# Packed attention and two feed-forwards on one core: a table moved, latents loaded once, and three pieces of work put in another order

## The chip, the core and the metric

One core of one Trainium2 chip runs the whole program. The metric is device time in microseconds (us) of one execution; 0.2% of it (3.5 us) is about what a measurement of this kernel can tell from no change. The engines are TensorE (PE; weight loads are listed apart as PEld), VectorE (DVE), ScalarE (ACT), GpSimd (POOL) and SyncE (SP), which here only issues DMAs, in the order in which the program writes them.

## The reference

```python
# q, k, v: (8, 8, 576, 64); p: (8, 8, 32, 64); all float32
p_packed = sm_attn(p, k, v)                 # 32 latents per head read 576 keys
out = sm_attn(q, p_packed, p_packed)        # 576 queries read the 32 latents
x = out.transpose(0, 2, 1, 3).reshape(4608, 512)
xn = x / sqrt(mean(x * x) + 1e-6) * rms_g   # first feed-forward, d_ff 1536
g = xn @ w_gate
x1 = (g * sigmoid(g) * (xn @ w_val)) @ w_out
h = x1 @ w_in                               # second feed-forward, d_ff 2048
return (h * cos(h)) @ w2_out
```

The weights arrive as 64-bit floats. The kernel narrows them itself: it loads each value as two 32-bit halves and puts a 32-bit float together from them (one ACT operation, then four DVE operations, or one of POOL and three of DVE).

## The kernel before

Every large product is made of three matmuls (helper `mm3`, L150 to L153): both operands are split into a rounded high part and the rest (`hilo`, L100 to L102: the high part on ACT, the rest on DVE), and high times high, high times low and low times high are added up in PSUM.

**Latent stage** (loop at L573, 18 steps `i`, two per batch and two to drain). Step i loads what later steps need (`load_k`: the latents p and the keys; `load_v`), transposes p and k on PE (`u_prep`, `u_kt`), makes scores, exponentials and the packed latents (`u_s1`, `u_e`, `u_et`, `u_pp`), and `u_fin` multiplies them by rms_g into `ppT` (L444). `u_prep` transposes a tile `pn` that holds p twice side by side; `load_k` fills both halves with a DMA each (L332, L333). Beside this each step loads weights (`w_load`, with `B0_L` for some more), narrows those loaded a step before (`w_prep`: part 0 is the ACT operation, part 1 the DVE ones), runs up to three steps of batch 0's attention (`bg0_step`, 34 of them, `attend(0)`), and at three steps builds a merged weight (`unit`). The last two narrowings, of weight pieces 14 and 15, stand at step 16, and the last `u_fin` at step 17. When the loop ends, its PSUM pools are handed over: the attention's transposes that follow (tile `atp`, L263) write banks that wait for the last reader of the old tiles.

**First feed-forward** (loop at L775). Per batch 24 steps `i`: `gv_block` (12 matmuls of 288 columns for gate and value, tiles `gv`), sigmoid on ACT, two products on DVE (`silu`, L675, L676), the split into `shl`, and two steps later `acc_block` (12 matmuls, tiles `acc`). Four PSUM tiles `mm` are shared by gate and value, the attention and the merged weights. Between these, `att_step` runs the next batch's attention in 41 small steps spread over the 48 half steps of a batch (for batch 0 from `ATT_FROM0` on), `U_AT` says after which step which merged weight `(batch, unit)` of batches 0 and 1 is built (16 matmuls `mps` into two tiles, two `hilo`s), and in batch 0 the remaining weights are narrowed: pieces 16 to 23 of gate and value in steps 0 to 8 and eight pieces of w_out by `WO_AT` in steps 1 to 18, with one operation of each on POOL (L131) and for w_out the low part on POOL too (L507). `wy_load` in that loop fetches three pieces ahead. The raw pieces and the finished w_out weights share the eight tiles of pool `wo1`.

**Second feed-forward** (loop at L910). 9 chunks of 512 tokens times 16 blocks f. `h_block`: 12 matmuls of 512 columns into one of four PSUM tiles `hp`, then a chain: kk on ACT (L868), three DVE operations (L869, L871, L872), absolute value and sine on ACT (L873, L874), the product with hp on DVE (L875, the last read of hp), and the split into `ghl` (ACT, DVE). Three blocks later `o_block` makes 12 matmuls of 512 columns (tiles `ops`).

**Order.** The latent stage and the first feed-forward are inside `order`, a region in which every engine runs its instructions in the order written. It is closed at L846, ahead of the second feed-forward, whose order a planner chooses by costs and readiness; the planner may put such instructions ahead of the last ones of the region.

**Addresses.** Pools are laid one behind the other in each partition. In the program as built, the pool `const` holds the identity, three small constants and the table `gT` of rms_g (32 bytes at byte 17120), and the resident weights `wm` start at 17152, followed by all other pools of the left side, the second feed-forward's included. The attention's operands `ahl`, `bdh` and the second feed-forward's moving operand `xhl` lie in pools at the right end, which are laid out from the other side (`ahl` at 222432, `bdh` at 218336, `xhl` at 196576 and 212960). 17152 is a multiple of 64; the three tiles on the right start 32 bytes off one.

Of the kernel before, what the change touches and what calls it, by code (L numbers as in the profile page):

```python
# [9 lines left out]
F32 = mybir.dt.float32  # L10
# [10 lines left out]
def kernel(  # L21
# [14 lines left out]
    nc = tc.nc  # L36
    B, H, S, D = q.shape
# [10 lines left out]
    NCK = FF1 // 256  # L48
    KD = DM // 128
    NG = 2 * B  # L50
# [14 lines left out]
    W_KV, W_B0 = 16, 16  # L65
    ATT_U, U_ATT = 34, 5
    U_S = {6: 0, 10: 1, 14: 2}
    U_AT = {1: (0, 3), 6: (0, 4), 10: (0, 5), 12: (1, 0), 14: (1, 1), 17: (1, 2), 19: (1, 3), 26: (1, 4), 29: (1, 5)}
    U_J = (16, 18, 20, 22, 25, 28)
    LATE_AT = 27  # L70
    B0_L = {15: (16,), 16: (17, -4), 17: (18,)}
    W_LOAD, W_SPLIT = (12, 13, 17, 18, 21, 22), (16, 17, 20, 21)
    W2_I0, W2_AT, W2_POOL = 28, (1, 3, 5, 7, 11, 14, 18), False
    T_END, F3_B = 2, 3
    LAG, LAG_B = 2, 3
    WO_AT = {4: (-1, 1), 5: (0, 3), 6: (3, 6), 7: (6, 9), 8: (9, 11), 9: (10, 13), 10: (13, 15), 11: (14, 17)}
    ATT_ORD = "t00 t01 x00 x01 x02 x03 t10 r00 t11 s00 x10 x11 p00 x12 p01 x13 - r10 - s10 - p10 p11"
    ATT_ORD0 = "t00 t01 x00 x01 x02 x03 r00 s00 t10 t11 x10 x11 x12 x13 r10 s10 p00 p01 p10 p11"
    AL_AT = 16
    ATT_FROM, ATT_TO, ATT_FROM0, N_ATT = 0, 48, 0, 43  # L80
    BX, BS, BW = 0, 3, 6

    wide = w_gate.dtype != F32
# [1 line left out]
    const = ctx.enter_context(tc.tile_pool(name="const", bufs=1))  # L85
# [89 lines left out]
    ps_1 = pst.enter_context(tc.tile_pool(name="ps_1", bufs=1, space=PSUM))  # L175

    top, bot = slice(0, 64), slice(64, 128)
    gT = const.tile([128, H], F32, name="gT")
    ppT = [pp_p.tile([128, H, 128], F32, tag=f"pp{i}", name=f"ppT{i}") for i in range(B // 4)]
    pT = u1.tile([128, 4, 160], F32, name="pT")  # L180
    nc.gpsimd.memset(pT, 0.0)
# [145 lines left out]
    def load_k(i):  # L327
        if i >= NG:
            return
        b, g = divmod(i, 2)  # L330
        pn = u2.tile([128, 2, D], F32, tag="pn", name="pn", bufs=4)
        for r in range(2):  # L332
            nc.sync.dma_start(out=pn[:, r], in_=p[b, 4 * g:4 * g + 4].rearrange("h n d -> (h n) d"))  # L333
        kn = u5.tile([128, CH * NC_, D], F32, tag="kn", name="kn", bufs=4)
        nc.sync.dma_start(out=kn, in_=k[b, 4 * g:4 * g + 4].rearrange("h (p c) d -> (h p) c d", c=CH * NC_))
        nat_k[i] = pn, kn
# [19 lines left out]
    def u_prep(i):  # L356
        pn, kn = nat_k.pop(i)
        z = st[i] = {}
        pt = ps_2.tile([128, 128], F32, tag="kp", name="pt")
        nc.tensor.transpose(pt, pn.rearrange("p a d -> p (a d)"), ident)  # L360
        nc.vector.tensor_copy(pT[:, :, :NP], pt.rearrange("p (h n) -> p h n", h=4))
        z["kT"], z["kn"] = u1.tile([128, 4, HALF], F32, tag="kT", name="kT"), kn
# [104 lines left out]
    def w_prep(n, part):  # L467
        if n >= W_KV:
            wo_prep(n - W_KV, u1, part)
            return  # L470
        wy_prep(n, part)
# [57 lines left out]
    def store(keep):  # L529
        while len(stores) > keep:  # L530
            dst, src = stores.pop(0)
            nc.sync.dma_start(out=dst, in_=src)
# [37 lines left out]
    u_prep(0)  # L570
    u_kt(0, range(CH))
    w_q, wo_q = [], []
    for i in range(NG + 2):  # L573
        due = list(w_due(i))
        for n in due:
            w_load(n)
        load_k(i + 4)
        for n in B0_L.get(i, ()):
            (wy_load if n >= 0 else wo_load)(abs(n))
        if i == 1:  # L580
            load_q()
            load_q()
        store(0)
        if i == U_ATT:
            att_load(0)
        if 0 < i <= NG:
            u_et(i - 1)
        if i < NG:
            u_s1(i)
        if i + 1 < NG:  # L590
            u_prep(i + 1)
            u_kt(i + 1, [0, 1])
        if 1 < i:
            u_fin(i - 2)
        if i < NG:
            u_e(i)
        if i + 1 < NG:
            u_kt(i + 1, [2])
        for n in w_q:
            w_prep(n, 0)  # L600
        for n in wo_q:
            wo_split(n - W_KV, 0)
        bg0_step(i, 1)
        if 0 < i <= NG:
            u_pp(i - 1)
        if i in U_S:
            unit(0, U_S[i])
        bg0_step(i, 0 if i == U_ATT else 2)
        for n in w_q:
            w_prep(n, 1)  # L610
        for n in wo_q:
            wo_split(n - W_KV, 1)
        wo_q = [n for n in w_q if n >= W_KV]
        w_q = due
        load_v(i + 2)
    store(0)
    assert not w_q and not wo_q and att_done[0] == ATT_U
    pst.close()
    ust.close()
# [155 lines left out]
    for i in range(len(seq) + LAG):  # L775
# [15 lines left out]
        if i >= LAG:  # L791
            acc_block(*seq[i - LAG])
            att_step(2 * i + 1)
            b, hf, f = seq[i - LAG]
# [25 lines left out]
            wy_prep(n - 1, 1)  # L820
        if n < 4 * NCK:
            wy_prep(n, 0)
            if n + 3 < 4 * NCK:
                wy_load(n + 3)
        for n, (at, to) in WO_AT.items():
            if at == i:
                wo_load(n)
# [15 lines left out]
            w2_narrow(len(w2_items) > 0)  # L843
    assert not wm_next
    assert not w2_items and not w2_raw
    order.close()  # L846
    fst.close()


# [11 lines left out]
    def h_block(n, f):  # L861
        w = wm_t["w", f // 2][f % 2]
        x = x_t[n][1]
        hp = ps_h.tile([128, TOK], F32, tag="h", name="hp")
        for d in range(KD):
            mm3(hp, w[:, 0, d], w[:, 1, d], x[:, 0, d], x[:, 1, d], d == 0, d == KD - 1)
        kk = b2.tile([128, TOK], F32, tag="kk", name="kk")
        nc.scalar.activation(out=kk, in_=hp, func=AF.Identity, scale=1.0 / TWO_PI, bias=magic[:, 0:1])  # L868
        nc.vector.tensor_scalar(out=kk, in0=kk, scalar1=-MAGIC, scalar2=None, op0=ALU.add)  # L869
        r = b3.tile([128, TOK], F32, tag="r", name="r")  # L870
        nc.vector.scalar_tensor_tensor(out=r, in0=kk, scalar=-PI_HI, in1=hp, op0=ALU.mult, op1=ALU.add)  # L871
        nc.vector.scalar_tensor_tensor(out=r, in0=kk, scalar=-PI_LO, in1=r, op0=ALU.mult, op1=ALU.add)  # L872
        nc.scalar.activation(out=r, in_=r, func=AF.Abs)  # L873
        nc.scalar.activation(out=r, in_=r, func=AF.Sin, scale=-1.0, bias=halfpi[:, 0:1])  # L874
        nc.vector.tensor_tensor(out=r, in0=r, in1=hp, op=ALU.mult)  # L875
        g = g_t[n, f] = b3.tile([128, 2, TOK], F32R, tag="ghl", name="ghl", bufs=LAG_B + 1)
        hilo(r, g[:, 0], g[:, 1])
# [32 lines left out]
    for i in range(len(seq) + LAG_B):  # L910
        if i < len(seq):
            n, f = seq[i]
            late_x = 2 * (n == 0)
            if f == 10 + late_x and n + 1 < NCH:
                load_x(n + 1)
            if f in (12 + late_x, 14 + late_x // 2) and n + 1 < NCH:
                split_x(n + 1, f // (14 + late_x // 2))
            if n == 0 and f in (3, 5, 9, 11):
                wm_split(wm_p if f < 6 else b4, nc.vector)
            if n == 0 and f in (3, 5):  # L920
                wm_load(("w", NCK + f // 4))
            h_block(n, f)
        if LAG_B <= i < len(seq) + LAG_B - T_END:
            n, f = seq[i - LAG_B]
            o_block(n, [f])
# [32 lines left out]
```

## Time and profile before

| what | value |
|---|---|
| median of 3 runs | 1765.15 us (1764.19 to 1766.03) |
| the profiled execution | 1766.95 us |
| its span on the core | 1765.2 us |
| PE busy / DVE busy | 1691.8 us (96%) / 1118.9 us (63%) |
| latent stage until the first gv matmul | 0 to 166.88 us |
| first feed-forward, batch 0 | 166.88 to 286.33 us |
| first feed-forward, batches 1 and 2 | 97.7 and 97.8 us each |
| first hp matmul of the second feed-forward | 953.63 us |

Times inside the trace count from the first instruction of the span; the execution's own time is 1.75 us longer. A row of the waits says which engine and line stood idle, what released it, the total, how often and the longest. A row of the windows view gives, for one stretch, its length and then the busy time of PE, PEld, DVE, ACT and POOL with the number of instructions, the granted clock of TensorE as a share of the full 2.4 GHz, the share of the DMA engines and GB/s.

### The profile page before, as it was taken

What the parts mean: (1) busy time and instruction counts of PE and PEld (TensorE: products, weight loads), DVE (VectorE), ACT (ScalarE), POOL (GpSimd) and SP (SyncE); (2) the same over time, 40 slices, a digit from 0 to 9 for tenths busy, and PEclk for the clock granted to TensorE, in tenths of its full rate; (3) what the DMA queues carried; (4) which work ended last, traced back from release to release, by engine and by line L of the source; (5) the groups of instructions that cost most, each with busy time, mean ns of one, the idle gap of its engine ahead of it and who ended that gap; (6) DMA issues with size and microseconds to landing.
All of it is one profiled execution on the core that took longest, in us unless ns stands there. A gap on an engine that the chain in (4) does not pass through costs nothing.

```text
span 1765.2 us, 28275 instructions
## 1 busy us (share of the span) xinstructions
PE 1691.8 (96%) x11184; PEld 1456.1 (82%) x11184; DVE 1118.9 (63%) x2184; ACT 833.2 (47%) x1597; POOL 61.6 (3%) x61
## 2 busy tenths in 40 slices
PE   7777789999999999999999999999999999999998
PEld 5555779989999999999898888888888888888887
DVE  3576876768677676866556655555555555555554
ACT  4454443444444444444446554545454545454443
POOL 0000421000000000000002000000000000000000
PEclk9887999999999999999999999999999999999999
DMA  9996443344453535241334100000000000000000
GB/s 257 264 257 180 146 140 116 111 154 142 150 172 132 178 104 195 100 143 38 111 108 147 35 27 22 25 25 24 25 24 25 24 25 25 25 1 25 0 25 24
DMA packets 90564, 165.42 MB, mean 94 GB/s; under 512 B 26432, under 2 KB 48960, under 8 KB 90432
## 3 DMA queue, kind: packets, MB, share of 16 engines
q1 hardware_dynamic: 90432, 163.62, 29.8%
q8 instruction: 88, 1.44, 0.4%
q14 instruction: 44, 0.36, 0.1%
HBM read 128.45 MB, written 35.13 MB: 93 GB/s over the span
## 4 chain that ended last, share of the span: by engine, by line
PE 82%; DVE 6%; DMA 5%; ACT 3%; issue 3%; SPq 1%; POOL 1%; DVEq 0%; ACTq 0%; POOLq 0%
PE hp L151 8%; PE hp L152 8%; PE hp L153 8%; PE ops L151 7%; PE ops L152 7%; PE ops L153 7%; PE gv L151 5%; PE acc L151 5%; PE acc L152 5%; PE acc L153 5%; PE gv L152 5%; PE gv L153 5%; PE mps L519 2%; PE sp L231 1%; DMA wo<-in_moe_w_val_dram 1%
## 5 line engine op out<-in xcount | busy, mean ns | idle before, releaser
L151 PE MATMUL gv<-apt,wmhl 128*128 128x288 f32 x768 | 237.4, 309 | 10.9 <-DVE silu L675 7.6
L151 PE MATMUL acc<-shl,wohl 128*128 128x288 f32 x768 | 234.7, 306 | 6.2 <-ACT x L708 5.7
L151 PE MATMUL hp<-xhl,wmhl 128*128 128x512 f32 x576 | 229.2, 398 | 3.8 <-DVE r L875 3.8
L152 PE MATMUL hp<-xhl,wmhl 128*128 128x512 f32 x576 | 228.9, 397 | 0.0
L153 PE MATMUL hp<-xhl,wmhl 128*128 128x512 f32 x576 | 228.6, 397 | 0.0
L152 PE MATMUL acc<-shl,wohl 128*128 128x288 f32 x768 | 228.0, 297 | 0.2 <-DVE shl L102 0.2
L153 PE MATMUL acc<-shl,wohl 128*128 128x288 f32 x768 | 228.0, 297 | 0.0
L152 PE MATMUL gv<-apt,wmhl 128*128 128x288 f32 x768 | 227.2, 296 | 0.0
L153 PE MATMUL gv<-apt,wmhl 128*128 128x288 f32 x768 | 226.6, 295 | 0.0
L152 PE MATMUL ops<-w2hl,ghl 128*128 128x512 f32 x576 | 225.7, 392 | 0.0
L151 PE MATMUL ops<-w2hl,ghl 128*128 128x512 f32 x576 | 225.7, 392 | 0.0
L153 PE MATMUL ops<-w2hl,ghl 128*128 128x512 f32 x576 | 223.2, 389 | 0.0
L875 DVE TENSOR_TENSOR r<-r,hp 128x512 f32<-128x512 f32 x144 | 98.9, 687 | 186.8 <-ACT r L874 186.6
L873 ACT ACTIVATE r<-r 128x512 f32<-128x512 f32 x144 | 90.9, 631 | 245.9 <-DVE r L872 245.9
L101 ACT ACTIVATE shl<-silu 128x288 fp32r<-128x288 f32 x192 | 85.2, 444 | 234.7 <-DVE silu L676 232.6
L151 PEld LDWEIGHTS gv<-apt,wmhl 128*128 128x128 f32 x768 | 144.8, 188 | 52.4 <-DVE silu L675 12.0
L868 ACT ACTIVATE kk<-hp,magic 128x512 f32<-128x512 f32 x144 | 99.0, 688 | 143.4 <-PE hp L153 143.2
L151 PEld LDWEIGHTS acc<-shl,wohl 128*128 128x128 f32 x768 | 145.0, 189 | 6.7 <-ACT x L708 5.9
L869 DVE TENSOR_SCALAR kk<-kk 128x512 f32<-128x512 f32 x144 | 61.4, 426 | 138.7 <-ACT kk L868 138.5
L152 PEld LDWEIGHTS acc<-shl,wohl 128*128 128x128 f32 x768 | 145.6, 190 | 0.5 <-DVE shl L102 0.4
L153 PEld LDWEIGHTS acc<-shl,wohl 128*128 128x128 f32 x768 | 145.1, 189 | 0.0
L152 PEld LDWEIGHTS gv<-apt,wmhl 128*128 128x128 f32 x768 | 145.0, 189 | 0.0
(125 smaller groups left out, 3029.0 us busy)
## 6 DMA issues: line engine op xcount, KB each, us to landing
wy<-wy SPq DMA_DIRECT2D x96, 512.0 KB, 4.3
kn<-in_k_dram SPq DMA_DIRECT2D x16, 576.0 KB, 6.2
vn<-in_v_dram SPq DMA_DIRECT2D x48, 192.0 KB, 5.7
qnat<-in_q_dram SPq DMA_DIRECT2D x32, 288.0 KB, 5.0
x_dram<-x SPq DMA_DIRECT2D x32, 288.0 KB, 2.8
x1raw<-x_dram SPq DMA_DIRECT2D x18, 512.0 KB, 4.2
raw<-in_moe_w_in_dram SPq DMA_DIRECT2D x16, 512.0 KB, 5.6
raw<-in_moe_w_out_dram SPq DMA_DIRECT2D x16, 512.0 KB, 5.3
```

The costliest lines, as they stand in the source:

```text
L101: nc.scalar.activation(out=hi, in_=src, func=AF.Copy)
L151: nc.tensor.matmul(ps, lhi, rhi, start=first, stop=False)
L152: nc.tensor.matmul(ps, lhi, rlo, start=False, stop=False)
L153: nc.tensor.matmul(ps, llo, rhi, start=False, stop=last)
L231: nc.tensor.matmul(sp[:, i, 2 * c:2 * c + 2, :], qT[:, i, c * CP:(c + 1) * CP], bq[:, 2 * j + i], start=True, stop=True,)
L519: nc.tensor.matmul(ps[kt][h * NP:(h + 1) * NP], ppT[b // 4][rows, 4 * kt + h, n:n + NP], w_y[2 * u + kt][rows, j], start=True, stop=True,)
L868: nc.scalar.activation(out=kk, in_=hp, func=AF.Identity, scale=1.0 / TWO_PI, bias=magic[:, 0:1])
L869: nc.vector.tensor_scalar(out=kk, in0=kk, scalar1=-MAGIC, scalar2=None, op0=ALU.add)
L873: nc.scalar.activation(out=r, in_=r, func=AF.Abs)
L875: nc.vector.tensor_tensor(out=r, in0=r, in1=hp, op=ALU.mult)
```

## The change

- `gT` moves from the pool `const` to `u1`, a pool of the latent stage. `const` is 32 bytes shorter; `wm` and all that lies behind it on the left start 32 bytes earlier (`wm` at 17120).
- `load_k` loads the latents once, into the first half of `pn`; `u_prep` copies them into the second half on POOL.
- Part 1 of the narrowings of step 16 (pieces 14 and 15, eight DVE operations) is written at step 17, behind the last `u_fin`.
- `B0_L` loads pieces 16, 17, 18 one step earlier, and pieces 19 and w_out 5 at step 17; the first feed-forward's loop then fetches four pieces ahead.
- `ATT_FROM0` goes from 0 to 10: during batch 0, the attention of batch 1 starts at half step 10 and is spread over the remaining 38.
- `U_AT`: unit (0, 3) is built after step 3 instead of 1; units (1, 0) to (1, 5) after steps 18, 21, 24, 26, 28, 30 instead of 12, 14, 17, 19, 26, 29.
- `order` stays open into the second feed-forward, until step `OWN` = 6. `h_block` ends at the sine; the product with hp and the split are a new function `h_rest`, which up to step 6 is written one block later, behind the next block's chain.

```diff
-    U_AT = {1: (0, 3), 6: (0, 4), 10: (0, 5), 12: (1, 0), 14: (1, 1), 17: (1, 2), 19: (1, 3), 26: (1, 4), 29: (1, 5)}
+    U_AT = {3: (0, 3), 6: (0, 4), 10: (0, 5), 18: (1, 0), 21: (1, 1), 24: (1, 2), 26: (1, 3), 28: (1, 4), 30: (1, 5)}
-    B0_L = {15: (16,), 16: (17, -4), 17: (18,)}
+    B0_L = {14: (16,), 15: (17,), 16: (-4, 18), 17: (19, -5)}
-    T_END, F3_B = 2, 3
+    T_END, F3_B, OWN = 2, 3, 6
-    WO_AT = {4: (-1, 1), 5: (0, 3), 6: (3, 6), ...
+    WO_AT = {4: (-1, 1), 5: (-1, 3), 6: (3, 6), ...
-    ATT_FROM, ATT_TO, ATT_FROM0, N_ATT = 0, 48, 0, 43
+    ATT_FROM, ATT_TO, ATT_FROM0, N_ATT = 0, 48, 10, 43
-    gT = const.tile([128, H], F32, name="gT")
+    gT = u1.tile([128, H], F32, name="gT")
...
-        for r in range(2):
-            nc.sync.dma_start(out=pn[:, r], in_=p[b, 4 * g:4 * g + 4].rearrange("h n d -> (h n) d"))
+        nc.sync.dma_start(out=pn[:, 0], in_=p[b, 4 * g:4 * g + 4].rearrange("h n d -> (h n) d"))
...
         z = st[i] = {}
+        nc.gpsimd.tensor_copy(pn[:, 1], pn[:, 0])
...
         if 1 < i:
             u_fin(i - 2)
+        w_late()
...
-        for n in w_q:
-            w_prep(n, 1)
-        for n in wo_q:
-            wo_split(n - W_KV, 1)
+        def w_late(ns=tuple(w_q), os=tuple(wo_q)):
+            for n in ns:
+                w_prep(n, 1)
+            for n in os:
+                wo_split(n - W_KV, 1)
+        if i < NG:
+            w_late()
+            w_late = lambda: None
...
-            if n + 3 < 4 * NCK:
-                wy_load(n + 3)
+            if n + 4 < 4 * NCK:
+                wy_load(n + 4)
...
-    order.close()
     fst.close()
...
         nc.scalar.activation(out=r, in_=r, func=AF.Sin, scale=-1.0, bias=halfpi[:, 0:1])
+        h_q[n, f] = r, hp
+
+    h_q = {}
+
+    def h_rest(n, f):
+        r, hp = h_q.pop((n, f))
         nc.vector.tensor_tensor(out=r, in0=r, in1=hp, op=ALU.mult)
...
             h_block(n, f)
+            if 0 < i <= OWN:
+                h_rest(*seq[i - 1])
+            if i == OWN:
+                order.close()
+            if i >= OWN:
+                h_rest(n, f)
```

## Rows read from the trace of the kernel before

**Rows 1.** Waits of PE, whole span: total us, times, longest.
```profile
PE acc L151 <- ACT x L708: 5.7, 1, 5.7
```
**Rows 2.** Windows by stage: columns as told above.
```profile
0.00:76.27 76.27, 53.79 (x655) 38.98 (x655) 33.85 (x88) 33.74 (x79) 2.34 (x13) 0.94 0.97 259
166.88:232.86 65.98, 52.73 (x396) 46.52 (x394) 55.20 (x101) 31.62 (x66) 22.61 (x15) 0.93 0.52 158
232.86:286.33 53.47, 51.21 (x403) 45.29 (x404) 40.45 (x91) 23.94 (x56) 14.16 (x11) 1.00 0.37 124
286.33:384.04 97.71, 97.05 (x806) 90.95 (x805) 66.15 (x145) 42.57 (x95) 1.82 (x2) 1.00 0.38 126
953.63:978.32 24.69, 20.94 (x86) 16.82 (x85) 18.88 (x33) 16.67 (x28) 0.00 (x0) 0.86 0.41 129
```
**Rows 3.** Timeline, SP at the start: start us, us, engine, line, tiles.
```profile
0.73 0.89 SPq L333 DMA_DIRECT2D pn<-in_p_dram  x2
```
**Rows 4.** Timeline, end of the latent stage; in brackets idle time and releaser.
```profile
160.15 0.42 DVE L137 TENSOR_SCALAR wy<-wy 128x512 f32<-128x512 f32 x1
...
164.04 0.69 DVE L146 SCALAR_TENSOR_TENSOR wy<-wo,wy 128x512 int32<-128x512 int32 x1
164.65 0.28 DVE L444 TENSOR_TENSOR ppT<-tp,gT 128x128 f32<-128x128 f32 x1
...
164.99 2.18 PE L263 MATMUL atp<-ident,s 96*128 96x96 f32 x12 [6.62 <-DVE ppT L444]
...
166.88 0.59 PE L151 MATMUL gv<-apt,wmhl 128*128 128x288 f32 x1
```
**Rows 5.** Timeline, batch 0, steps 3 to 6: POOL, DVE, ACT and PE.
```profile
187.05 1.68 POOL L131 TENSOR_SCALAR wy<-wy 128x512 f32<-128x512 f32 x1 [4.53 <-ACT wy L129]
187.42 0.98 DVE L143 SCALAR_TENSOR_TENSOR wy<-wo,wy 128x512 int32<-128x512 int32 x1
...
190.30 0.66 ACT L129 ACTIVATE ny<-wo 128x512 f32<-128x512 f32 x1 [2.81 <-POOL wohl L507]
...
197.56 0.40 PE L151 MATMUL gv<-apt,wmhl 128*128 128x288 f32 x1 [2.00 <-DVE silu L675]
```
**Rows 6.** Groups by shape, whole span: count | busy us, mean ns | idle before.
```profile
L519 PE MATMUL mps<-wy,ppT 64*32 64x512 f32 x768 | 56.5, 604 | 1.7 <-DVE silu L675 0.8 <-ACT qT L225 0.5 <-ACT sq L291 0.3
...
L255 DVE TENSOR_TENSOR s<-s,sm 96x768 f32<-96x768 f32 x16 | 15.1, 946 | 0.0
L251 DVE TENSOR_REDUCE sm<-s 96x24 f32<-96x768 f32 x16 | 15.1, 942 | 0.0
```
**Rows 7.** Timeline, start of the second feed-forward, ACT and PE.
```profile
967.52 1.28 ACT L874 ACT_TABLE_LOAD   x1
...
970.31 0.80 PE L151 MATMUL hp<-xhl,wmhl 128*128 128x512 f32 x1 [3.75 <-DVE r L875]
...
975.52 0.39 PE L151 MATMUL hp<-xhl,wmhl 128*128 128x512 f32 x1
```
**Rows 8.** Timeline, one steady block: first matmuls of hp, ops, hp; then ACT.
```profile
1103.01 0.40 PE L151 MATMUL hp<-xhl,wmhl 128*128 128x512 f32 x1
...
1105.81 0.39 PE L151 MATMUL ops<-w2hl,ghl 128*128 128x512 f32 x1
...
1108.56 0.40 PE L151 MATMUL hp<-xhl,wmhl 128*128 128x512 f32 x1
...
1106.01 0.69 ACT L868 ACTIVATE kk<-hp,magic 128x512 f32<-128x512 f32 x1 [1.05 <-PE hp L153]
1106.60 0.62 ACT L101 ACTIVATE ghl<-r 128x512 fp32r<-128x512 f32 x1
...
1109.78 0.72 ACT L874 ACTIVATE r<-r,halfpi 128x512 f32<-128x512 f32 x1
```
**Rows 9.** Groups by shape, whole span: 288-column matmuls, operands on the left (gv), right (xp).
```profile
L152 PE MATMUL gv<-apt,wmhl 128*128 128x288 f32 x768 | 227.2, 296 | 0.0
...
L152 PE MATMUL xp<-ahl,bdh 128*128 128x288 f32 x64 | 18.8, 294 | 0.0
```

More of the change, by code (lines that the diff above doesn't have):

```diff
@@ L67 @@
     U_S = {6: 0, 10: 1, 14: 2}
-    U_AT = {1: (0, 3), 6: (0, 4), 10: (0, 5), 12: (1, 0), 14: (1, 1), 17: (1, 2), 19: (1, 3), 26: (1, 4), 29: (1, 5)}
+    U_AT = {3: (0, 3), 6: (0, 4), 10: (0, 5), 18: (1, 0), 21: (1, 1), 24: (1, 2), 26: (1, 3), 28: (1, 4), 30: (1, 5)}
     U_J = (16, 18, 20, 22, 25, 28)
     LATE_AT = 27
-    B0_L = {15: (16,), 16: (17, -4), 17: (18,)}
+    B0_L = {14: (16,), 15: (17,), 16: (-4, 18), 17: (19, -5)}
     W_LOAD, W_SPLIT = (12, 13, 17, 18, 21, 22), (16, 17, 20, 21)
     W2_I0, W2_AT, W2_POOL = 28, (1, 3, 5, 7, 11, 14, 18), False
-    T_END, F3_B = 2, 3
+    T_END, F3_B, OWN = 2, 3, 6
     LAG, LAG_B = 2, 3
-    WO_AT = {4: (-1, 1), 5: (0, 3), 6: (3, 6), 7: (6, 9), 8: (9, 11), 9: (10, 13), 10: (13, 15), 11: (14, 17)}
+    WO_AT = {4: (-1, 1), 5: (-1, 3), 6: (3, 6), 7: (6, 9), 8: (9, 11), 9: (10, 13), 10: (13, 15), 11: (14, 17)}
     ATT_ORD = "t00 t01 x00 x01 x02 x03 t10 r00 t11 s00 x10 x11 p00 x12 p01 x13 - r10 - s10 - p10 p11"
@@ L608 @@
         bg0_step(i, 0 if i == U_ATT else 2)
-        for n in w_q:
-            w_prep(n, 1)
-        for n in wo_q:
-            wo_split(n - W_KV, 1)
+        def w_late(ns=tuple(w_q), os=tuple(wo_q)):
[5 more added lines that the diff above has]
+            w_late()
+            w_late = lambda: None
         wo_q = [n for n in w_q if n >= W_KV]
@@ L616 @@
     store(0)
+    w_late()
     assert not w_q and not wo_q and att_done[0] == ATT_U
```

## The prediction

> **What bounds the kernel now.** I read the windows by stage first, then the waits of PE, then the timelines around each place that the diff touches. PE is busy for 96% of the span, so a change can win only what PE stands idle or what it runs slowly. The windows say where that is [rows 2]. From 0 to 76.27 PE is busy 53.79 of 76.27 us, and the DMA engines are busy at a share of 0.97: the loads set the pace. From 166.88 to 232.86 (first half of batch 0) DVE is busy 55.20 of 65.98 and PE 52.73, and the longest wait of PE in the whole span, 5.7 us, lies there: an `acc` matmul waits until the old `acc` has been copied out, and that copy stands on ACT behind a split that waits for DVE [rows 1]. From 232.86 to 286.33 PE is busy 51.21 of 53.47: PE sets the pace again, and batch 1 is full (97.05 of 97.71). Batch 0 takes 65.98 + 53.47 = 119.45, so 21.7 more than batch 1. The last weak stretch is the start of the second feed-forward, 953.63 to 978.32: granted clock 0.86, PE busy 20.94 of 24.69. What follows is bound by PE: the steady block goes from one `hp` to the next in 5.55 us, and its `hp` and `ops` parts are back to back [rows 8].
>
> **The change part by part.**
>
> *Latents loaded once.* Sixteen DMAs go, each 128x64 in float32, 32 KB. Thirteen of them are issued in the stretch at 0.97 and 259 GB/s [rows 2]. 13 x 32 KB at that rate is 0.43 MB / 259 GB/s = 1.6 us; I take -1.6. The bounds are 0 (the removed bytes were not what PE waited for) and the time that SP needs to issue them, 0.89 us for two [rows 3], 13 x 0.45 = -5.8. The copy that is added on POOL is shown by no row. POOL is busy 2.34 of those 76.27 us [rows 2], the latents are loaded several steps ahead of `u_prep`, and only the first copy has nothing ahead of it; there kn, loaded behind it, is late too. Its cost is between 0 and, for the first step alone, 1.68 (the longest POOL row of eight times the size [rows 5]); I take 0, since DMA still sets that stretch. If the cover went, each copy would delay a transpose by its length.
>
> A row speaks on what the copies do to DVE: beside a POOL operation of 1.68 us DVE's L143 took 0.98 us [rows 5], where an undisturbed operation of this kind and size took 0.69 [rows 4], so 0.29 more. The Trainium skill, *SBUF — State Buffer*, section *Who interferes with whom*, goes further: the port pair that DVE and GpSimd share is an exclusive lock, so that an operation which needs it stands still until the other engine is done. By that rule a copy would stop DVE for its whole length, the sum would lose this part's 1.6 us and little more, because DVE is idle for over half of that stretch; by the row it loses nothing. The row bears out an interference, and not a standstill (1.31 us of the POOL operation were still to run when L143 began).
>
> *Last narrowing later.* Eight DVE operations run from 160.15 to 164.73, and the `ppT` product L444 comes behind them at 164.65; the tile `atp` waits for it, and PE is idle for 6.62 us until 164.99 [rows 4]. Written behind the last `u_fin`, the narrowing no longer holds L444, which could start at about 160.2, and `atp` 0.34 later, 4.4 us earlier. The same 4.6 us of DVE then stand ahead of the low parts of `apt`, for which the first `gv` waits. They end at 160.15 + 0.28 + 4.58 = 165.0, and one low part has to follow, at most the 0.69 of a 512-column operation [rows 4], say 0.6: first `gv` at 165.6 instead of 166.88. I take -1.3; the bounds are 0 and -4.4. The next thing late is DVE itself.
>
> *Batch 0: attention and merged weights later.* By half step 24 the old spread asks for 43x24//48 = 21 attention steps, the new one for 43x14//38 = 15. With those six leave two reductions and two products on DVE, 2 x (0.942 + 0.946) = 3.8 us [rows 6], from the half that is bound by DVE. They return in the second half, where DVE has 13.0 us to spare and PE 2.3 [rows 2]. I take -3.8. At most the 5.7 us wait [rows 1] goes as well: -9.5. Two units leave batch 0 and return in batch 1, at 56.5/48 = 1.18 us of PE each [rows 6]: -2.4 where PE sets the pace and +2.4, so 0; if batch 0 doesn't give them back, +2.4. Units (1, 3) and (1, 5) end two steps ahead of their first use. ACT's wait for POOL (2.81) and the POOL operations are not touched [rows 5]. The earlier loads pass other loads on SP's queue. A piece is 128x512x8 bytes = 0.52 MB, 2.0 us at 259 GB/s; DMA is at 0.52 there [rows 2] and no ACT wait in batch 0 ends with a DMA in these rows. I take 0, with +2.0 as a bound if a load that PE needs is pushed back, and 0 as the other (nothing waited for them).
>
> *Start of the second feed-forward in written order.* In before the planner put `hp` blocks ahead; the fifth waits for the L875 of the first at 969.57 and PE stands for 3.75 us. Twelve matmuls then take 975.52 - 970.31 = 5.21 us [rows 7] at the lower clock (0.86 as the mean of the stretch [rows 2]), against 2.80 in a steady block [rows 8]: 2.41 lost, together 6.2. In written order the last `acc` comes ahead of the first `hp`, at 953.63 before; that is 12 matmuls, 12 x 97.05/806 = 1.4 us [rows 2]. Four `hp` follow from about 955.0 on, back to back, until 955.0 + 4 x 2.80 = 966.2. The chain from kk to the end of the sine takes 1109.78 + 0.72 - 1106.01 = 4.49 in the steady state, of which 0.5 is a split operation of another block [rows 8]. So the first kk begins at about 958.0 and the first sine ends at 958.0 + 4.0 + 1.28 (table load [rows 7]) = 963.3. The new `h_rest` stands behind the second chain, whose kk waits on ACT behind that first sine: 963.3 + 4.0 = 967.3, then the split on ACT (0.62) and DVE (about as long): the first `ops` can run at about 968.5. That leaves one stall of 2.3 us, which I take; two weight splits (steps 3 and 5) stand in the same queues. Who waits: ACT's kk of the next block behind each split, and PE behind the low part. After that a block asks ACT and DVE for less than PE's 5.55 [rows 8], so the stall does not come again. Does it lower the clock? A wait of 2.00 at 197.56 was followed by a 288-column matmul of 0.40 [rows 5], not of 0.59 as at the lower clock after the 6.62 [rows 4]; the 3.75 was followed by the low clock [rows 7]. So -6.2 - 0.3 (a short wait in the last `acc`) + 2.3 = -4.2. Bounds: -2.5 (each split stalls PE for another 0.8) and -6.5 (no stall).
>
> *Addresses.* Everything on the left moves by 32 bytes, to 32 off a multiple of 64. In before `hp` has one operand on the right (`xhl`, 32 off) and takes 2.80, `ops` has both on the left and takes 2.75 [rows 8]: 0.05 for each of 144 blocks, 7.2 us. The 288-column matmuls with both operands on the right, `xp`, take 294 ns, those with both on the left, `gv`, 296 [rows 9]: being 32 bytes off cost those nothing. I take 0, nearest to that row, with -7.2 and +7.2 as bounds.
>
> **Sum.** -1.6 - 1.3 - 3.8 - 4.2 + 0 = -10.9 on the profiled execution of 1766.95, so 1756.05. That execution lay 1.8 above the median of 1765.15, so **1754.2** on the median.
>
> **The rivals.**
> - *Operands alike are fast.* If `hp` is slow because its two operands lie differently, both now lie 32 off, and it falls to the rate of `ops`: -7.2, so 1747.0. For it speaks that `ops` and `xp`, with like operands, are the fast ones; against it that many other things differ between `hp` and `ops`. Chance 0.14.
> - *32 off is slow for 512 columns only.* `ops` then rises to the rate of `hp`: 1761.4, hardly measurable. Chance 0.08.
> - *Slower: 32 off is slow for each matmul on the left.* The difference is 0.05/12 = 4.2 ns for a matmul. Over the 192 x 24 = 4608 of the first feed-forward and the 1728 of `ops` that is 26.4 us: 1754.2 + 26.4 = 1780.6. It is slower than before from 10.9/6336 = 1.7 ns on. Row 294 against 296 speaks against it [rows 9]. Chance 0.07.
> - *DVE stays the bound of batch 0, and the written order stalls.* The narrowing stays in the first half, and POOL's single tile still holds ACT [rows 5]; batch 0 gives 0 and the start 2.5: 1765.15 - 1.6 - 1.3 - 2.5 = 1759.8. Chance 0.13.
>
> On the three rivals with addresses: rows show the difference of 0.05 and none at 288 columns. The Trainium skill, *Advanced Engine Details and Errata*, section *SBUF Cachelines*, gives lines of 16 bytes, and by that a shift of 32 bytes changes nothing, so that the sum would be the forecast's; no run here shows it yet.
>
> **How the numbers follow.** Forecast (1749 to 1758, the sum with one or two terms at their bounds): chance 0.58. The range: 1747.0 must be in, 1759.8 too, and the slower rival stays out; 1745 to 1762. What a measurement of this kernel can tell from no change is about 0.2%, 3.5 us, so faster means under 1761.6. Faster: 0.58 + 0.14 + most of 0.13 = 0.83; same: most of 0.08 and the rest of 0.13 = 0.10; slower 0.07.
>
> **What would show it.** Right: the wait ahead of the first `atp` is under 1 us instead of 6.62, while the first `gv` comes only 1 to 2 us earlier for it; the first 76 us shrink by 1 to 2; the wait of 5.7 shrinks, batch 0 takes 114 to 116, batch 1 about 100; at the first `ops` there is one wait near 2 us with the granted clock at 1.00, and no run of matmuls at half rate; `hp` and `ops` stay at 2.80 and 2.75. Wrong: another step of `hp`, `ops` or `gv` (addresses); a wait for a merged weight at step 28 or 32 (units too late); a table load or split that stalls PE in each of the first six blocks; a batch 0 that is as long as before.

## The result and the profile after

The changed kernel takes 1751.08 us (median; 1749.49 to 1754.51) against 1765.59 for the kernel before measured beside it. The ratio is 0.9915, 95% interval 0.989 to 0.994, so it is faster by 14.5 us; 1754.2 was forecast. The profiled execution has a span of 1749.6 us, 15.6 shorter than before. The total came out near the forecast, but not by the terms of the forecast. By stage, from the starts in the two traces:

| stretch | before | after | difference |
|---|---|---|---|
| latent stage, to the first gv | 166.88 | 166.96 | +0.1 |
| batch 0 | 119.46 | 119.80 | +0.3 |
| batch 1 | 97.71 | 100.20 | +2.5 |
| batches 2 to 6 | 488.32 | 489.58 | +1.3 |
| first gv of batch 7 to the end | 892.81 | 873.08 | -19.7 |

So all of the gain, and more, lies in the last stretch, and the three edits that were to help before it gave together nothing in these two profiles. (The 1.3 of batches 2 to 6 lies within their spread: over all the kernels below these batches take 488.3 to 491.4.) The windows of the changed kernel, with the columns of [rows 2] (first 76 us, the two halves of batch 0, batch 1, first hp to first ops, and the 18 us behind that):

```profile
0.00:76.27 76.27, 57.31 (x661) 41.39 (x662) 30.97 (x82) 33.60 (x80) 5.39 (x24) 0.89 1.01 252
166.96:229.72 62.76, 53.57 (x385) 49.86 (x385) 48.69 (x91) 28.40 (x61) 22.52 (x15) 0.85 0.48 150
229.72:286.76 57.04, 52.12 (x382) 48.81 (x381) 43.37 (x98) 25.92 (x57) 14.46 (x11) 0.91 0.26 87
286.76:386.96 100.20, 99.56 (x838) 91.55 (x837) 68.05 (x149) 44.60 (x99) 1.82 (x2) 1.00 0.44 143
958.96:971.67 12.71, 11.06 (x50) 8.82 (x48) 5.62 (x11) 6.75 (x11) 0.00 (x0) 1.00 0.13 46
971.67:990.00 18.33, 18.33 (x80) 14.86 (x81) 13.99 (x24) 12.05 (x21) 0.00 (x0) 1.00 0.17 59
```

The first half of batch 0 did become shorter, 62.76 instead of 65.98, with 6.5 us less on DVE. The second half became longer by as much: 57.04 instead of 53.47, at a granted clock of 0.91 instead of 1.00. The waits of PE over the whole span, those of the latent stage among them, say what stands in batch 0 now (total, times, longest):

```profile
PE gv L151 <- DVE silu L682: 9.1, 9, 2.5
PE et L411 <- ACT e L399: 7.9, 4, 5.4
PE sp L231 <- ACT qT L225: 7.7, 4, 3.8
...
PE gv L151 <- DVE apt L102: 4.1, 1, 4.1
PE atp L263 <- DVE s L255: 3.6, 1, 3.6
```

The wait of 5.7 for the copied `acc` [rows 1] is gone. In its place PE waits twice for batch 1's own attention, whose products and transposes stand in PE's written order ahead of the next blocks: once in the first half of batch 0, for 3.76 us, and once in the second, for 3.64. The timeline of PE at these two places, and at the next gv block behind the second:

```profile
214.33 1.22 PE L231 MATMUL sp<-bq,qT 128*96 128x64 f32 x6 [3.76 <-ACT qT L225]
...
238.32 0.74 PE L263 MATMUL atp<-ident,s 96*128 96x96 f32 x3 [3.64 <-DVE s L255]
...
243.23 0.61 PE L151 MATMUL gv<-apt,wmhl 128*128 128x288 f32 x1 [0.75 <-DVE silu L682]
243.63 0.44 PE L152 MATMUL gv<-apt,wmhl 128*128 128x288 f32 x1
243.87 0.44 PE L153 MATMUL gv<-apt,wmhl 128*128 128x288 f32 x1
```

Behind the wait of 3.64 the matmuls follow each other at 0.24 us and are recorded with 0.44, the lower of the two clock levels (granted clock 0.50 from 238.32 to 246.00); the mean of this shape over the whole span before is 0.296 [rows 9].

The end of the latent stage (compare [rows 4]): the first six `atp` follow at once, the next wait 0.91 for the normalised attention, and the first gv waits 4.12 for the low part of `apt`.

```profile
159.14 0.67 PE L298 MATMUL rp<-ones,ssq 128*96 128x1 f32 x6 [2.22 <-DVE ssq L292]
...
159.81 0.66 PE L263 MATMUL atp<-ident,s 96*128 96x96 f32 x6
161.38 1.47 PE L263 MATMUL atp<-ident,s 96*128 96x96 f32 x6 [0.91 <-DVE s L309]
166.96 0.61 PE L151 MATMUL gv<-apt,wmhl 128*128 128x288 f32 x1 [4.12 <-DVE apt L102]
```

At the start of the second feed-forward (compare [rows 7]) the wait of 3.75 and the slow stretch are gone. There is one wait, 1.65 us, ahead of the first ops, and the granted clock is 1.00 ahead of it and behind it (the last two windows above):

```profile
971.67 0.50 PE L151 MATMUL ops<-w2hl,ghl 128*128 128x512 f32 x1 [1.65 <-ACT ghl L101]
...
974.81 0.39 PE L151 MATMUL hp<-xhl,wmhl 128*128 128x512 f32 x1
```

And the steady block itself is shorter, in every one of its matmuls. The groups by shape of the kernel before (count | busy us, mean ns):

```profile
L151 PE MATMUL hp<-xhl,wmhl 128*128 128x512 f32 x576 | 229.2, 398 | 3.8 <-DVE r L875 3.8
L152 PE MATMUL hp<-xhl,wmhl 128*128 128x512 f32 x576 | 228.9, 397 | 0.0
...
L152 PE MATMUL ops<-w2hl,ghl 128*128 128x512 f32 x576 | 225.7, 392 | 0.0
```

and of the changed one:

```profile
L151 PE MATMUL hp<-xhl,wmhl 128*128 128x512 f32 x576 | 224.1, 389 | 0.0
L152 PE MATMUL hp<-xhl,wmhl 128*128 128x512 f32 x576 | 224.1, 389 | 0.0
...
L152 PE MATMUL ops<-w2hl,ghl 128*128 128x512 f32 x576 | 224.1, 389 | 0.0
```

From first matmul to first matmul, the medians over the blocks after 1000 us: `hp` 2.802 and `ops` 2.744 before, both 2.720 after. That is 5.546 - 5.440 = 0.106 for a block, 15.3 us for 144.

### The profile page after: what moved, and what is told of

Same layout as the page of the kernel before. It is cut to its first block, busy times and chain, and to the rows that moved or that the text cites. A ratio compares the mean times of both kernels' runs of the same rounds, so it can differ in the third digit from the quotient of the medians.

```text
span 1749.6 us, 28297 instructions
## 1 busy us (share of the span) xinstructions
PE 1682.0 (96%) x11184; PEld 1463.1 (84%) x11184; DVE 1116.9 (64%) x2184; ACT 835.6 (48%) x1599; POOL 67.5 (4%) x77
## 4 chain that ended last, share of the span: by engine, by line
PE 80%; DMA 6%; DVE 5%; issue 4%; ACT 3%; POOL 1%; SPq 0%; DVEq 0%; ACTq 0%; POOLq 0%
PE ops L153 7%; PE ops L151 7%; PE ops L152 7%; PE hp L151 7%; PE hp L152 7%; PE hp L153 7%; PE gv L151 5%; PE acc L151 5%; PE acc L152 5%; PE acc L153 5%; PE gv L152 5%; PE gv L153 5%; DMA kn<-in_k_dram 3%; PE mps L519 2%; PE sp L231 1%
## 5 line engine op out<-in xcount | busy, mean ns | idle before, releaser
L151 PE MATMUL hp<-xhl,wmhl 128*128 128x512 f32 x576 | 224.1, 389 | 0.0
L152 PE MATMUL hp<-xhl,wmhl 128*128 128x512 f32 x576 | 224.1, 389 | 0.0
L153 PE MATMUL hp<-xhl,wmhl 128*128 128x512 f32 x576 | 224.1, 389 | 0.0
L151 PEld LDWEIGHTS gv<-apt,wmhl 128*128 128x128 f32 x768 | 146.7, 191 | 54.1 <-DVE silu L682 13.3
L152 PEld LDWEIGHTS gv<-apt,wmhl 128*128 128x128 f32 x768 | 147.3, 192 | 0.0
L153 PEld LDWEIGHTS gv<-apt,wmhl 128*128 128x128 f32 x768 | 146.9, 191 | 0.0
```

The lines of the kernel that those rows point to most:

```text
L151: nc.tensor.matmul(ps, lhi, rhi, start=first, stop=False)
L152: nc.tensor.matmul(ps, lhi, rlo, start=False, stop=False)
L153: nc.tensor.matmul(ps, llo, rhi, start=False, stop=last)
```

## The experiments

Two questions had to be told apart first: is the shorter block due to the addresses, or to the new written order? And why did batch 0 not become shorter?

**Only the table back in its old place.** The changed kernel with

```diff
-    gT = u1.tile([128, H], F32, name="gT")
+    gT = const.tile([128, H], F32, name="gT")
```

> The changed kernel with one part undone: gT is back in the pool const, so everything on the left lies 32 bytes higher again, as in the kernel before; all else of the change stays. The changed kernel's steady block of the second feed-forward takes 2.72 (hp) + 2.72 (ops) us instead of 2.80 + 2.74, about 0.10 us over 144 blocks, 15 us. Theory 'addresses': the 32 bytes do that, so here the block is at 2.80 + 2.74 again and the time is about 1751 + 15 = 1766. Rival 'order': the order written for the start, or the product and the split in a function of their own, changed the steady order, so the block stays at 2.72 + 2.72 and the time at 1751.

Measured: ratio to the kernel before 0.997 (0.9959 to 0.998), 1762.15. The block is at 2.802 + 2.744 again. The time is below the 1766 of the expectation because the written start is still in: its one wait ahead of the first ops is 1.42 here, and from batch 7 to the end it takes 888.1, 4.7 less than before.

**Only the table moved.** The kernel before with the same line changed the other way round; the instructions of every engine are the same and in the same order.

> The kernel before with one part of the change: gT lies in the pool u1 instead of const, nothing else. Theory 'addresses': the block of the second feed-forward falls from 2.80 + 2.74 to 2.72 + 2.72, and the time from 1765.6 to about 1750; batches of 288-column matmuls get no longer by more than 0.2 us each. Rival 'order': no change, 1765.6.

Measured: ratio 0.9928 (0.9911 to 0.9944), 1754.11. The block is at 2.720 + 2.720, and from batch 7 to the end it takes 877.0 instead of 892.8. Its hp matmuls, 397 ns before, take:

```profile
L152 PE MATMUL hp<-xhl,wmhl 128*128 128x512 f32 x576 | 224.7, 390 | 0.0
```

The rival "order" falls with these two kernels: moving a table by itself, with no instruction changed, is worth 12.7 us by the ratio and 15.8 by the trace.

**Batch 0 in the old order.** The changed kernel with

```diff
-    U_AT = {3: (0, 3), 6: (0, 4), 10: (0, 5), 18: (1, 0), 21: (1, 1), 24: (1, 2), ...
+    U_AT = {1: (0, 3), 6: (0, 4), 10: (0, 5), 12: (1, 0), 14: (1, 1), 17: (1, 2), ...
-    ATT_FROM, ATT_TO, ATT_FROM0, N_ATT = 0, 48, 10, 43
+    ATT_FROM, ATT_TO, ATT_FROM0, N_ATT = 0, 48, 0, 43
```

> The changed kernel with the old spread of batch 0's attention steps (from half step 0) and the old places of the merged weights; all else of the change stays. In the changed kernel batch 0 takes 119.8 us, as long as before, and its granted clock fell from 0.93 and 1.00 in its two halves to 0.86 and 0.90. Theory 'density': the attention, squeezed into 38 half steps, makes PE wait for its own chain (at 214 and 238 us, 3.8 and 3.6), each wait with a stretch at the lower clock behind it, and that eats what DVE gained; here those waits go, the second half is at 1.00 again, batch 0 is no longer than 119.8, batch 1 returns from 100.2 to 97.7, and the time is about 1748.5. Rival 'DVE' (the forecast's term): the later order does relieve DVE by 3.8 us, so here batch 0 takes about 123.5 and the time is about 1752.5.

Measured: ratio 0.9905 (0.9885 to 0.9924), 1750.79: the whole time can't tell 1748.5 from 1752.5. The windows of its batch 0 (two halves) and batch 1 can:

```profile
165.06:231.94 66.88, 55.23 (x394) 48.82 (x394) 55.03 (x101) 29.56 (x63) 22.62 (x15) 0.89 0.47 147
231.94:285.42 53.48, 51.27 (x404) 45.41 (x405) 40.43 (x91) 23.96 (x56) 14.16 (x11) 1.00 0.36 123
285.42:383.54 98.12, 97.11 (x807) 91.01 (x806) 66.11 (x145) 42.73 (x95) 1.82 (x2) 1.00 0.39 126
```

Against the changed kernel the first half is 4.1 longer, so the forecast's relief of DVE is real there. The second half is 3.6 shorter and back at 1.00, and batch 1 is 2.1 shorter. In sum the two batches take 218.5 instead of 220.0: the new order costs 1.5. That is the theory "density", though batch 0 by itself (120.35) is half a us longer than it expected, and the wait of 5.7 for the copied `acc` is back in it: the new order had traded this one wait for the two of 3.76 and 3.64. The spread of the attention and the places of the merged weights were undone together; which of the two costs batch 0 how much is not shown.

**The planner's start again.** The changed kernel with the region closed ahead of the second feed-forward:

```diff
+    order.close()
     fst.close()
...
             h_block(n, f)
-            if 0 < i <= OWN:
-                h_rest(*seq[i - 1])
-            if i == OWN:
-                order.close()
-            if i >= OWN:
-                h_rest(n, f)
+            h_rest(n, f)
```

> The changed kernel with the region of written order closed ahead of the second feed-forward, as before, and the product and split written with their own block. Forecast's term for the written start: 4.2 us. So the 3.75 us wait ahead of the fifth hp and the slow stretch behind it return, and the time is about 1755. The steady block stays at 2.72 + 2.72 by the theory 'addresses', and goes back to 2.80 + 2.74 (time about 1770) by the rival 'order'.

Measured: ratio 0.9957 (0.9943 to 0.9972), 1760.02. The wait ahead of the fifth hp is back with 3.92 us, the block stays at 2.720 + 2.720, and from batch 7 to the end it takes 878.1, 5.0 more than the changed kernel. The whole time is 2 to 4 us more again than that (by the ratios or by the medians). The profiled execution, the slowest of the eight at 1764.79, shows a likely reason: its first gv came at 174.51, 7.5 later than in the changed kernel's profile, though nothing ahead of it is written differently. How long the latent stage was in the other seven is not on record. That spread needs its own look. The first two windows of 20 us of this kernel:

```profile
0.00:20.00 20.00, 12.93 (x116) 9.44 (x116) 2.96 (x10) 7.24 (x16) 2.99 (x16) 1.00 0.94 193
20.00:40.00 20.00, 13.30 (x166) 10.01 (x167) 6.21 (x19) 7.01 (x18) 0.71 (x3) 0.81 1.02 232
```

and of the one with the table back, whose latent stage is written the same but for the 32 bytes of address, and whose first gv came at 161.76:

```profile
0.00:20.00 20.00, 13.62 (x116) 9.91 (x116) 2.83 (x9) 6.96 (x14) 3.46 (x18) 1.00 0.93 244
20.00:40.00 20.00, 18.66 (x271) 13.94 (x265) 10.46 (x30) 11.01 (x30) 0.47 (x2) 1.00 1.06 275
```

The DMA engines are as busy in both, but moved 193 and 232 GB/s in the one and 244 and 275 in the other; the changed kernel itself lies between, with 226 and 257. The rate of the loads differs from execution to execution, and of these three the stage ends the later the lower it is. A term of 1 or 2 us in this stage can't be read from one profile.

**Addresses and start alone.** The kernel before with `gT` in `u1` and the written start; latents, narrowing, loads and batch 0 as before.

```diff
-    gT = const.tile([128, H], F32, name="gT")
+    gT = u1.tile([128, H], F32, name="gT")
...
-    order.close()
     fst.close()
...
             h_block(n, f)
+            if 0 < i <= OWN:
+                h_rest(*seq[i - 1])
+            if i == OWN:
+                order.close()
+            if i >= OWN:
+                h_rest(n, f)
```

> The kernel before with two parts of the change: gT in u1 (addresses), and the start of the second feed-forward in written order; latents loaded twice, the last narrowing, batch 0's order and the loads as before. By the traces so far the addresses are worth 15.5 us and the start 4.8, together 20.3, a ratio of 0.9885 to the kernel before. Theory 'the rest gives nothing': this is as fast as the whole change or up to 5 us faster. Rival 'the rest is worth its forecast' (1.6 + 1.3 + 3.8): it is about 6 us slower than the whole change, ratio about 0.995.

**The changed kernel again**, with no edit, beside it.

> The changed kernel once more, to stand beside the others of this call on the same chip. Ratio to the kernel before as measured first, 0.9915. The first gv lay at 162 to 175 us in four kernels whose latent stage is the same but for one address, so a profile of the same kernel may show it some us away from 167 too.

Measured: 0.9911 (0.9896 to 0.9926) for the two parts, 0.9929 (0.9911 to 0.9948) for the whole change. The rest of the change, then, gives nothing that these intervals can tell; the rival expected 0.995 for the two parts alone. In the trace of the two parts batch 0 takes 119.49 and batch 1 97.78; in the repeated whole 119.77 and 100.21, as in its first profile.

**Latents twice.** The changed kernel with

```diff
-        nc.sync.dma_start(out=pn[:, 0], in_=p[b, 4 * g:4 * g + 4].rearrange("h n d -> (h n) d"))
+        for r in range(2):
+            nc.sync.dma_start(out=pn[:, r], in_=p[b, 4 * g:4 * g + 4].rearrange("h n d -> (h n) d"))
...
-        nc.gpsimd.tensor_copy(pn[:, 1], pn[:, 0])
```

> The changed kernel with the latents loaded twice again and without the copy on POOL; all else as changed. Forecast's term: the sixteen loads are worth 1.6 us (between 0 and 5.8), so this is 1.6 us slower than the changed kernel of the same call, and the sixth transpose of pn comes at about 35 us as in the kernel before, against 33.7 to 34.3 in two of the changed ones. Rival: the rate of DMA, which differs from execution to execution, decides, and the two are equal within 1 us; with a copy that held DVE, this would be faster.

Measured: 0.9926 (0.9911 to 0.9941), equal to the whole change measured beside it (0.9929). The sixth transpose of `pn` starts at 35.9 here and at 34.9 to 36.3 in all eight profiles with two loads; with one load it starts at 33.7 to 34.7 in five and at 43.7 in the one with the slow loads. That is about one us by there, where 1.6 was forecast for the stage; by the end of the stage the spread has swallowed it. The term is not settled.

**Narrowing early.** The changed kernel with

```diff
-        if i < NG:
-            w_late()
-            w_late = lambda: None
+        w_late()
+        w_late = lambda: None
```

> The changed kernel with the last narrowing back at step 16, ahead of the last u_fin; all else as changed. From the end of the last wait for ssq (the start of the rp matmuls) to the first gv it takes 9.35 us in the kernel before and 7.82 in the changed one: here 9.35, the 6.62 us wait ahead of atp is back, the wait of 4.1 ahead of the first gv is gone. Theory 'clock': the late narrowing moves the stretch at the lower clock onto the first gv matmuls and gives back 0.8 of the 1.5, so here batch 0 is about 0.8 us shorter and the time 0.7 longer than the changed kernel. Rival (forecast): batch 0 is the same, 1.5 longer.

Measured: 0.9908 (0.9892 to 0.9924). Both theories expected it to be slower, and 9.35 us from the start of the rp matmuls to the first gv. It takes 7.91, close to the 7.82 of the changed kernel, and not the 9.35 of before. The timeline of PE shows why:

```profile
160.19 0.95 PE L263 MATMUL atp<-ident,s 96*128 96x96 f32 x3 [0.90 <-DVE s L309]
165.41 0.74 PE L263 MATMUL atp<-ident,s 96*128 96x96 f32 x3 [4.28 <-DVE ppT L444]
165.86 0.59 PE L151 MATMUL gv<-apt,wmhl 128*128 128x288 f32 x1
```

Only the last three of the twelve `atp` wait for L444, where in [rows 4] all twelve did. In the kernel with latents loaded twice but narrowed late, it is the other way round:

```profile
164.79 2.18 PE L263 MATMUL atp<-ident,s 96*128 96x96 f32 x12 [2.12 <-DVE ppT L444]
169.65 0.61 PE L151 MATMUL gv<-apt,wmhl 128*128 128x288 f32 x1 [2.68 <-DVE apt L102]
```

There rp to gv takes 7.82. In the programs as built the last `tp`, which L444 reads, lies in PSUM bank 4 where the latents are loaded twice and in bank 5 where they are loaded once; the first `atp` tile takes bank 4 and the fourth bank 5. The two parts without either edit (addresses and start alone) take 9.35 again, with all twelve `atp` behind a wait of 6.62. So each of two edits, the late narrowing and, by a side effect on the banks, the single load, buys the same 1.5 us, and the second of them buys nothing more.

**Where must the two sides lie?** Four kernels change the kernel before by unused bytes alone: `padl`, a tile of the stated size in `const`, moves the left side up, `padr`, 32 bytes in a pool opened first on the right, moves the right side down. Each adds one memset; in the third the table is moved as well, in the fourth `padl` has 16 columns. For the first and the second:

```diff
+    padl = const.tile([128, 8], F32, name="padl")
+    nc.gpsimd.memset(padl, 0.0)
     make_identity(nc, ident)
```

```diff
+    padr = ctx.enter_context(tc.tile_pool(name="padr", bufs=1, side="right")).tile([128, 8], F32, name="padr")
+    nc.gpsimd.memset(padr, 0.0)
     ast = ExitStack()
```

> The kernel before with 32 unused bytes more in const: everything on the left 32 bytes higher, at 32 off a multiple of 64 (as in the changed kernel, but 64 bytes further up); the right side as before, also 32 off. Theory 'rest of 64': only the place within 64 bytes counts, so the block is at 2.72 + 2.72 and the time about 15 us below before. Rival 'the place itself': another step, for instance 2.80 + 2.74, and no gain.

> The kernel before with 32 unused bytes at the right end: xhl, ahl, bdh 32 bytes lower, now at a multiple of 64, like everything on the left. Theory 'alike': hp is slow because its operands lie differently; here both lie alike, hp falls to 2.72 or at least to the 2.74 of ops, and the time by 8 to 12 us. Rival 'left': what counts is where the left side lies (the tiles that ACT and DVE read and write beside PE among it), so hp stays near 2.80 and the time at that of before.

> The kernel before with gT in u1 (left side at 32 off) and 32 unused bytes at the right end (right side at a multiple of 64): operands of hp unlike again, the other way round. Theory 'alike': hp at about 2.80 and ops at 2.72, so the time is 3 to 4 us below before. Rival 'left': hp and ops at 2.72, time 15 us below before.

> The kernel before with 64 unused bytes more in const: the left side stays at a multiple of 64, 64 bytes higher. Theory 'rest of 64': nothing changes, 2.80 + 2.74, time of before. Rival 'the place itself' (or a period of 128 bytes): other steps.

Measured, with the addresses of the first `wmhl` and `xhl` tiles as built (the tiles of a pool lie 4096 or 16384 bytes apart):

| kernel | wmhl | xhl | xhl - wmhl | hp | ops | ratio to before |
|---|---|---|---|---|---|---|
| changed; table moved alone | 33504 | 196576 | 163072 | 2.720 | 2.720 | 0.9915; 0.9928 |
| before; table back | 33536 | 196576 | 163040 | 2.802 | 2.744 | 1; 0.997 |
| table moved, right down 32 | 33504 | 196544 | 163040 | 2.802 | 2.744 | 1.0016 (1.0005 to 1.0027) |
| left up 32 | 33568 | 196576 | 163008 | 2.800 | 2.740 | 1.0013 (1.0 to 1.0026) |
| right down 32 | 33536 | 196544 | 163008 | 2.800 | 2.740 | 0.9998 (0.9988 to 1.0008) |
| left up 64 | 33600 | 196576 | 162976 | 2.806 | 2.734 | 1.0014 (0.9999 to 1.0029) |

"Rest of 64" falls with "left up 32", "alike" with "right down 32" and "left up 32" (both sides alike, both slow), and "left" with "table moved, right down 32": its left side lies where that of the fast kernel does. What orders the table is the distance between the two sides. Of 163040 and 163008 there are two placements each, and both have the same two times; of four distances 32 bytes apart only 163072 is fast. (163072 itself stands in one placement only. It is a multiple of 256; whether that is what counts, or of which number, four distances don't say.) In the slow kernel "table moved, right down 32" the groups read as in the kernel before:

```profile
L151 PE MATMUL hp<-xhl,wmhl 128*128 128x512 f32 x576 | 228.9, 397 | 3.8 <-DVE r L877 3.8
...
L152 PE MATMUL ops<-w2hl,ghl 128*128 128x512 f32 x576 | 225.7, 392 | 0.0
```

A shift of one side moves all its tiles, also those that ACT, DVE or a DMA use beside PE. Two traces speak against these. In the kernel with the table back ACT, DVE and POOL stand idle for 1.10 us within the very first hp block, and the steps are as long as elsewhere: 956.11 - 955.17 = 0.94 for four, where the fast kernels take 0.91. A window of that stretch, and two rows of PE in it:

```profile
955.20:956.30 1.10, 1.10 (x6) 0.92 (x5) 0.00 (x0) 0.00 (x0) 0.00 (x0) 1.00 0.99 353
...
955.17 0.40 PE L153 MATMUL hp<-xhl,wmhl 128*128 128x512 f32 x1
...
956.11 0.40 PE L151 MATMUL hp<-xhl,wmhl 128*128 128x512 f32 x1
```

There the DMA engines were busy; in the kernel before they are idle during the hp part of [rows 8], which takes 2.80 all the same:

```profile
1103.01:1105.81 2.80, 2.80 (x13) 2.25 (x12) 1.21 (x2) 1.35 (x2) 0.00 (x0) 1.00 0.00 0
```

That leaves what PE itself reads in `hp`: the weights on the left and the moving tile on the right.

What stays open is the mechanism. `ops` reads nothing on the right, and yet its first five matmuls are slow when the distance is a slow one; here is an ops part of the kernel before:

```profile
1105.81 0.39 PE L151 MATMUL ops<-w2hl,ghl 128*128 128x512 f32 x1
...
1106.97 0.39 PE L153 MATMUL ops<-w2hl,ghl 128*128 128x512 f32 x1
...
1108.33 0.39 PE L153 MATMUL ops<-w2hl,ghl 128*128 128x512 f32 x1
1108.56 0.40 PE L151 MATMUL hp<-xhl,wmhl 128*128 128x512 f32 x1
```

The first five steps take 1106.97 - 1105.81 = 1.16, 0.232 each, the last seven 1108.56 - 1106.97 = 1.59, 0.227 each, the rate of the changed kernel. The changed kernel shows the same five steps too, in its first hp block, behind the last `acc` and its 288 columns:

```profile
958.96 0.39 PE L151 MATMUL hp<-xhl,wmhl 128*128 128x512 f32 x1
...
960.11 0.39 PE L153 MATMUL hp<-xhl,wmhl 128*128 128x512 f32 x1
...
961.70 0.39 PE L151 MATMUL hp<-xhl,wmhl 128*128 128x512 f32 x1
```

Again 1.15 for five steps, then 1.59 for seven. So five such steps don't need a slow `hp` ahead of them. That they are how a stretch settles which follows one of another spacing, and that a slow `hp` never settles, is a reading, not shown.

## Why the prediction was right, and where it was not

That the total lay only 3 us from the forecast is luck, since its errors had opposite signs: the addresses gave 15 us more, the latent stage (forecast -2.9, measured +0.1) and batches 0 and 1 (forecast -3.8, measured +2.8) together 9.6 less. One reading of rows was wrong without consequence: the wait of 5.7 us is the longest of the first feed-forward, not of the whole span, where the 6.62 of [rows 4] is longer.

*Addresses (0 forecast, bounds 7.2 either way).* Measured 15 us: 15.8 with the table moved alone, 15.0 between the changed kernel and the one with the table back. The rival that had named a gain there, at a chance of 0.14, had its sign right, its size at half and its reason wrong: kernels with like operands are slow too. The two rivals in which 32 bytes off is slow fell as well: hp and ops are both faster, and the batches of 288-column matmuls did not get longer. The step that failed is the bound. It took the 2.75 of `ops` [rows 8] as the fast rate, while 5 of its 12 matmuls were slow as well; the seven rows behind them, at 0.227, would have given 2 x 12 x 0.227 = 5.45 for a block instead of 5.55, and a bound of 0.10 x 144 = 14.4. The row for which 0 was chosen, 294 against 296 ns [rows 9], was no evidence: each of those matmuls has both operands on one side, so that their distance could not change. The page weighed there (the Trainium skill, *Advanced Engine Details and Errata*, section *SBUF Cachelines*: lines of 16 bytes) would have had 32 bytes change nothing; the measurement decides, and they changed 15 us.

*Start of the second feed-forward (-4.2).* Right. The changed kernel takes 5.0 less from batch 7 on than with the planner's start; with the old addresses the two differ by 4.7. The stall at the first ops is 1.65 instead of 2.3, the clock stays at 1.00, and no later block shows a wait of over 0.4.

*Batch 0 (-3.8).* The direction was right for the half that it was worked out for: 3.2 less, with 6.5 us less on DVE where 3.8 were counted. The step that failed is "they return in the second half, where DVE has 13.0 us to spare and PE 2.3". It counted busy time, not waits: in written order PE stood ahead of one attention product (3.76 us, still in the first half) and one transpose (3.64, in the second) until the step before was done, and behind each it ran at the lower clock. 3.6 us came back in the second half, and batch 0 is as long as it was in every kernel of this study (119.3 to 120.4).

*Merged weights (0, bound +2.4).* The bound was the answer. Batch 1 takes 2.5 more wherever the new order stands, and batch 0 didn't give it back. No matmul waited for a merged weight at steps 28 or 32.

*Last narrowing (-1.3).* Alone it is worth what was forecast: with the latents loaded twice, rp to gv is 7.82 instead of 9.35, 1.5 shorter, and the first gv then waits for DVE's low part as foretold. But the step "the tile `atp` waits for it" (for L444) held only for the old bank; with the single load in, the move is worth nothing. An edit that was not thought to touch PSUM changed which tile waits.

*Latents once (-1.6).* Open. One us is seen by the sixth step, and the spread of the DMA rate hides the rest. POOL is busy 5.39 us of the first 76 instead of 2.34, and of a DVE that stands still beside the copies (the Trainium skill, *SBUF — State Buffer*, section *Who interferes with whom*) nothing is to be seen: no DVE operation beside a copy took over 0.05 us more than its like, and where a copy met a running L146 it was the copy that took longer, 0.73 us instead of 0.24.

```profile
45.16 0.69 DVE L146 SCALAR_TENSOR_TENSOR wy<-wo,wy 128x512 int32<-128x512 int32 x1
...
45.22 0.73 POOL L358 COPY pn<-pn 128x64 f32<-128x64 f32 x1 [9.61 <-DMA pn<-in_p_dram]
```

But that the rows show "an interference, and not a standstill" was read from one row. Beside another POOL operation of the kernel before, a DVE operation whose like take 0.46 us took 1.34:

```profile
217.62 1.26 POOL L507 TENSOR_TENSOR wohl<-ny,wohl 128x512 fp32r<-128x512 f32 x1 [3.74 <-ACT wohl L504]
...
217.86 1.34 DVE L102 TENSOR_TENSOR shl<-silu,shl 128x288 fp32r<-128x288 f32 x1
```

*Earlier loads (0).* No run undid them alone; with the old loads, narrowing and order batch 0 takes 119.49 instead of 119.80.

## What to carry to other kernels

In a steady stretch, read the spacing from matmul to matmul, not the mean of a block: if the same shape has two spacings, the shorter one may be what placement can give for all of them, and moving one side of the memory by a few bytes is an experiment of one line. When work is shifted out of a crowded half into a full one, price the waits that its chain has in written order there, and the slow clock behind them, not only its busy time. Where several edits meet at one wait, undo each alone: two of them may be buying the same time.

## What the runs showed of the hardware

- A 512-column matmul of this kernel starts every 0.227 us, or in an `hp` block every 0.233 to 0.234 in the mean, depending on the distance between the right side, where its moving tile lies, and the left side, where its weights lie: 2% of the second feed-forward for 32 bytes. The same distance gave the same two block times in two placements each (163040 and 163008).
- Waits of 3.64 and 3.76 us of PE were followed by matmuls at the lower clock level (granted clock 0.50 from 238.32 to 246.00 and from 214.33 to 219.35); the wait of 1.65 at the first ops was not, and the 18 us behind it have 1.00.
- The rate of the first 40 us of loads differed from 193 and 232 to 244 and 275 GB/s between two executions of a latent stage that was the same but for 32 bytes of address, with the DMA engines equally busy, and the first gv lay at 174.5 or at 161.8.
- Of a POOL copy and a DVE operation that overlapped, the copy took longer (0.73 us instead of 0.24) and the DVE operation did not; beside a longer POOL operation that had begun before it, a DVE operation took 1.34 us instead of 0.46.
